# A spectral filter and a low-rank mixer: the low-rank part of u on four row strips of TensorE, two groups at a time

## The chip, the cores and the metric

The kernel runs on one core of a Trainium2 chip. The metric is the device time of one execution in microseconds (us), median of several runs.

## The reference

x is 8 x 3136 x 256 (batch, sequence, channel). A real FFT along the sequence is multiplied by a complex filter and transformed back; then a low-rank mixing over the sequence and an MLP over the channels follow.

```python
X = np.fft.rfft(x, axis=1)
Y = X * (filt_r + 1j * filt_i)[None, :, :]
x = np.fft.irfft(Y, n=x.shape[1], axis=1)
...
xt = x.transpose(0, 2, 1)
h = xt @ U @ V                                  # rank 32
u = x + h.transpose(0, 2, 1)
ch = np.maximum(u @ w_ch1, 0.0) @ w_ch2         # 256 -> 1024 -> 256
return (u + ch).astype(np.float32)
```

## The kernel before

**The transform.** 3136 = 64 x 49. One batch's spectrum goes through four stages: `f1_units` (64-point transform, tile pf, written to DRAM), `load_a` (reads it back in four pieces of eight frequencies, tile a2), `stream` (per step two frequencies: px = transform over 49, products with the filter, pi = transform back, tile esb, to DRAM), and `load_e` (reads back, tile e2). The last 64-point transform is folded into the making of u: e2 is the stationary operand and the constant s2 is streamed. A step of `stream` is one px of two 256-column matmuls, three products on VectorE (`product`: uv, lines 454 and 456), an addition on GpSimd (y), and, two steps later, a pi of two 256-column matmuls with an eviction by ScalarE. Batch 0 goes through a version of its own ahead of everything (`first_f1`, `first_mid`), and the steps of batch 1 use `both_products` (one VectorE operation).

**The low-rank part.** `h1_unit(b)` forms h1 from e2 and the transformed U: 25 matmuls with 32 stationary columns each, on four column strips of TensorE in turn, so that the 128 rows of h1 hold four partial sums of the 32 ranks. `vr` (made once, by `v_units`) holds V four times, one copy per 32 rows. So one matmul over 128 rows with h1 as the stationary operand and vr streamed both adds the partial sums and multiplies by V.

**The mixer.** A batch is cut into groups of four sequence rows of 128 positions, r0 = 0, 4, ..., 20; the 25th half row of two batches makes one odd group after each odd batch. For a group `make_u` builds u, transposed, in two halves of 128 channels (dh): one matmul with h1 and vr, 512 columns, then four with e2 and s2, 128 columns each, all in one bank, evicted to a tile ut. `mm1(gx, t)` forms eighth t of the hidden layer (two 512-column matmuls, relu into h), `mm2(gx, rr)` forms the output of one row (eight matmuls of 256 columns with h as the stationary operand, two of 128 columns that add u), and after every second row VectorE copies it to och, which is written to the output.

**The order of the work** is written out by hand (`manual_schedule`), so each engine works through its instructions in the order of the program. The main loop runs over the groups gx. A group has four steps a; a step has two `mm1` calls (t = 2a, 2a + 1), `run(slot)`, at a = 2 the `make_u` of the next group, the `mm2` call of the group before (rr = a), and `run(slot + 1)`. So a group of four rows has 8 slots, a batch 48. `run` advances what `put` has set for that slot: steps of `stream` (every 1.5 slots for batch 1, 2.87 for batch 2, every 3 for the others: in a batch's own count slots 1, 4, 7, ... 28 and 31, 34, ... 46), pieces of `f1_units` (every 3 slots: 0, 3, ... 18 and 30, ... 45), loads, and `h1_unit` at slot 44. The steps run out in the second half of batch 6; batch 7's groups have none.

**Buffers.** PSUM has eight banks: one "x" (px), one "f" (pi and h1), four "m" (phh of `mm1`, pu of `make_u`, pf), two "o" (po of `mm2`). A bank is given out again when its reader has finished. In SBUF there are four a2, three ut, 18 h, two och. Lines to know: 506 (h1's eviction), 520 to 531 (`u_part`, lines 524 and 529), 544 to 554 (`make_u`), 556 to 568 (`mm1`; VectorE does the relu of t = 4, in the last batch of 1, 4 and 6, ScalarE the others), 570 to 600 (`mm2`), 435 (px), 252 (`v_units`: a 32-row matmul with the constant `sel`, which makes four copies).

The part of the main loop that sets the order:

```python
        for a in range(4):
            if live:
                mm1(gx, 2 * a)
                mm1(gx, 2 * a + 1)
            if full:
                run(slot)
            if a == 2 and gx + 1 < len(groups):
                nxt = groups[gx + 1][0]
                if nxt != groups[gx][0] and nxt % 2:
                    make_odd(nxt - 1)
                make_u(gx + 1)
            mm2(gx - 1, a)
            if full:
                run(slot + 1)
                slot += 2
```

Of the kernel before, what the change touches and what calls it, by code (L numbers as in the profile page):

```python
# [9 lines left out]
F16 = mybir.dt.float16  # L10
# [6 lines left out]
DM = 256  # L17
RANK = 32
ESC = 16.0
NH = 25  # L20
CH = [6, 6, 6, 7]
KG = 8
# [3 lines left out]
def _consts():  # L26
    n, half = SEQ, SEQ // 2
    r = np.arange(NR)
    q = np.arange(NQ)


    w = np.zeros((NQ, NS, 2))
    for s in range(NS):
        w[:, s, 0] = np.cos(2 * np.pi * s * q / NQ)
        w[:, s, 1] = -np.sin(2 * np.pi * s * q / NQ)
    w[:, 0, 1] = (-1.0) ** q
    w = w.reshape(NQ, 64)
    w64 = np.zeros((128, 128))
    w64[:64, :64] = w
    w64[64:, 64:] = w  # L40
    s2 = np.zeros((128, 128))
    s2[:64, :64] = w.T / ESC
    s2[64:, 64:] = w.T / ESC


    t2 = np.zeros((NS, 98, 128))
    g = np.zeros((NS, 128, 98))
    for s in range(NS):
        for j in range(49):
            if j < 25:  # L50
                f = s + 64 * j
                e, sg = np.exp(-2j * np.pi * f * r / n), 1.0
            elif s:
                f = 64 * (j - 24) - s
                e, sg = np.exp(-2j * np.pi * (n - f) * r / n), -1.0
            else:
                f = 32 + 64 * (j - 25)
                e, sg = np.exp(-2j * np.pi * f * r / n), 1.0
            ei = np.conj(e)
            if s:  # L60
                t2[s, :49, j], t2[s, 49:, j] = e.real, -e.imag
                t2[s, :49, 64 + j], t2[s, 49:, 64 + j] = sg * e.imag, sg * e.real
                g[s, j] = np.concatenate([ei.real, ei.imag]) * 2
                g[s, 64 + j] = np.concatenate([-ei.imag, ei.real]) * 2 * sg
            else:
                o = 0 if j < 25 else 49
                t2[s, o:o + 49, j] = e.real
                t2[s, o:o + 49, 64 + j] = e.imag
                g[s, j, o:o + 49] = ei.real * (2 if f else 1)
                g[s, 64 + j, o:o + 49] = -ei.imag * 2  # L70

    t2[0, :, 64] = 0
    t2[0, 49:, 64] = (-1.0) ** r
    g[0, 64] = 0
    g[0, 64, 49:] = (-1.0) ** r
    g *= ESC / n
    gs = np.concatenate([g[:, 64:], g[:, :64]], 1)
    f16 = np.float16
    return (w64.astype(f16), s2.astype(f16), np.eye(128).astype(f16),
            np.tile(np.eye(32), (1, 4)).astype(f16),  # L80
            np.ascontiguousarray(t2.transpose(1, 0, 2).reshape(98, NS * 128)).astype(f16),
            np.ascontiguousarray(np.stack([g, gs], 1).transpose(2, 0, 1, 3)
                                 .reshape(128, NS * 2 * 98)).astype(f16))
# [3 lines left out]
def kernel(  # L87
# [11 lines left out]
    nc = tc.nc  # L99
# [18 lines left out]
    def bank(tag, name):  # L118
        return ps.tile([128, 512], F32, tag=tag, bufs=BUFS[tag], name=name)
# [78 lines left out]
    load_rest()  # L198
    for c in range(2, len(CH)):
        load_x(0, c)  # L200
    sel = cst.tile([32, 128], F16)
    nc.sync.dma_start(sel, sel_d.ap())
    for k, part in enumerate(PARTS):
        if k == 3:
# [43 lines left out]
    def v_units():  # L248

        for r0, n, vp in vps:  # L250
            pv = bank("m", "pv")
            nc.tensor.matmul(pv[:, 0:n], sel[:, :], vp[:, 0:n], start=True, stop=True)
            nc.scalar.copy(vr[:, r0 * 128:r0 * 128 + n], pv[:, 0:n])
            yield

# [61 lines left out]
    def first_a(m):  # L317
        gi, ml = divmod(m, KG // 2)
        if ml == 0:
            st[0].setdefault("a", {})[gi] = sb.tile([98, KG * DM], F16, tag="a2", bufs=4, name="a2")  # L320
        pt = bank("o", "pt")
        for sl in range(2):
            for dh in range(2):
                o = sl * DM + dh * 128
                k = dh * 64 * NR + (2 * m + sl) * 98
                nc.tensor.matmul(pt[0:98, o:o + 128], at[:, k:k + 98], idn[:, :],
                                 start=True, stop=True, skip_group_check=True)
        nc.scalar.copy(st[0]["a"][gi][:, ml * 512:(ml + 1) * 512], pt[0:98, :])  # L328
# [87 lines left out]
        return bass.AP(tensor=t, offset=gi * KG * 2 * RD, ap=[[DM, 98], [2 * RD, KG], [1, DM]])  # L416

    def load_a(b, gi):
        t = sb.tile([98, KG * DM], F16, tag="a2", bufs=4, name="a2")
        nc.sync.dma_start(t.rearrange("p (k d) -> p k d", d=DM), spec(c1[b], gi))  # L420
        st[b].setdefault("a", {})[gi] = t

# [74 lines left out]
    def h1_unit(b):  # L497
        e2 = st[b]["e2"]
        ph = bank("f", "ph")
        for r in range(NH):  # L500
            j = 32 * (r % 4)
            nc.tensor.matmul(ph[j:j + 32, 0:DM], usb[:, r * RANK:(r + 1) * RANK],
                             e2[:, r * DM:(r + 1) * DM], start=(r < 4), stop=(r >= NH - 4),
                             tile_position=(0, j), skip_group_check=True)
        h1 = sb.tile([128, DM], F16, tag="h1", bufs=2, name="h1")
        nc.scalar.mul(h1, ph[:, 0:DM], 1.0 / ESC)  # L506
        st[b]["h1"] = h1
        yield

# [2 lines left out]
    groups = []  # L512
# [4 lines left out]
    uts, hs, pos, ochs = {}, {}, {}, {}  # L517
    odd = {}

    def u_part(b, r0, nr, half, pm, o, dh):  # L520

        e2, h1 = st[b]["e2"], st[b]["h1"]
        k = 64 if half else 128
        nc.tensor.matmul(pm[:, o:o + nr * k], h1[:, dh * 128:(dh + 1) * 128],  # L524
                         vr[:, r0 * 128:r0 * 128 + nr * k], start=True, stop=False,
                         skip_group_check=True)
        for rr in range(nr):
            a = (r0 + rr) * DM + dh * 128
            nc.tensor.matmul(pm[:, o + rr * k:o + (rr + 1) * k], e2[0:k, a:a + 128],  # L529
                             s2[0:k, 0:k], start=False, stop=(rr == nr - 1),  # L530
                             skip_group_check=True)

    def make_odd(b):
        if b % 2 == 0:
            odd[b // 2] = sb.tile([128, 256], F16, tag="odd", bufs=2, name="odd")
        pm = bank("m", "pu")
        for dh in range(2):
            u_part(b, NH - 1, 1, True, pm, dh * 64, dh)
        a = 64 * (b % 2)
        nc.scalar.copy(  # L540
            odd[b // 2].rearrange("p (h q) -> p h q", h=2)[:, :, a:a + 64],
            pm[:, 0:128].rearrange("p (h q) -> p h q", h=2))

    def make_u(gx):
        b, r0, nr = groups[gx]
        if nr == 1:
            make_odd(b)
            uts[gx] = odd[b // 2]
            return
        uts[gx] = sb.tile([128, 1024], F16, tag="ut", bufs=3, name="ut")  # L550
        for dh in range(2):
            pm = bank("m", "pu")
            u_part(b, r0, nr, False, pm, 0, dh)
            nc.scalar.copy(uts[gx][:, dh * 512:(dh + 1) * 512], pm)  # L554

    def mm1(gx, t):
        w = groups[gx][2] * 128
        ut = uts[gx]
        pm = bank("m", "phh")
        for dh in range(2):  # L560
            nc.tensor.matmul(pm[:, 0:w], w1[:, dh * 1024 + t * 128:dh * 1024 + (t + 1) * 128],  # L561
                             ut[:, dh * w:(dh + 1) * w], start=(dh == 0), stop=(dh == 1))
        h = sb.tile([128, 512], F16, tag="h", bufs=18, name="h")
        hs[gx, t] = h
        if t in ((4,) if groups[gx][0] < nb - 1 else (1, 4, 6)):
            nc.vector.tensor_relu(h[:, 0:w], pm[:, 0:w])  # L566
        else:
            nc.scalar.activation(h[:, 0:w], pm[:, 0:w], RELU)  # L568

    def mm2(gx, rr):  # L570
        if gx < 0 or rr >= groups[gx][2]:
            return
        b, r0, nr = groups[gx]
        w = nr * 128
# [29 lines left out]
    def put(slot, gen):  # L604
        sched.setdefault(int(slot + 0.5), []).append(gen)
# [22 lines left out]
    fill = f1_units(1, True)  # L628
    vgen = v_units()
    first_mid(fill)  # L630
    next(h1_unit(0))
    make_u(0)

    steps = [9 + 1.5 * k for k in range(NP)] + [33 + 2.87 * k for k in range(NP)]
# [9 lines left out]
    for b in range(1, nb):  # L644
        for gi in range(NS // KG):
            t = steps[NP * (b - 1) + GP * gi]
            put(t - 9, one(load_a, b, gi))
        put(SB * b - 4, h1_unit(b))
        if b > 1:
            fill = f1_units(b, b == 2)  # L650
            for k in range(NF):
# [4 lines left out]
                if b > 2:  # L656
                    put(steps[NP * (b - 1)] - 68 + 10 * c, one(load_x, b, c))

    for k in range((NH - 1) // 4):
        put(1 + 2 * k, vgen)  # L660

    slot = 0
    for gx in range(len(groups) + 1):
        live = gx < len(groups)
        full = live and groups[gx][2] == 4
        for a in range(4):
            if live:
                mm1(gx, 2 * a)
                mm1(gx, 2 * a + 1)
            if full:  # L670
                run(slot)
            if a == 2 and gx + 1 < len(groups):
                nxt = groups[gx + 1][0]
                if nxt != groups[gx][0] and nxt % 2:
                    make_odd(nxt - 1)
                make_u(gx + 1)
            mm2(gx - 1, a)
            if full:
                run(slot + 1)
                slot += 2  # L680
# [30 lines left out]
```

## Time and profile before

| | |
|---|---|
| median of 3 runs | 557.24 us (557.11 to 557.61) |
| the profiled execution: time, and span from first to last instruction | 560.07 us, 558.3 us |
| TensorE, matmuls (PE) | 529.5 us busy, 4450 matmuls |
| VectorE (DVE) | 366.9 us busy |
| ScalarE (ACT) | 363.1 us busy |
| GpSimd (POOL) | 248.8 us busy |
| mean granted clock of TensorE | 0.988 |

The table is the page's first part. Busy time of PE is the union of its matmuls, which are pipelined: a 512-column matmul lasts 0.379 us (L561) while the next starts earlier. How fast PE works is read from the starts in a timeline, and what it waits for from the pairs of a late start and the end of another engine's operation just before it. In a row of a group the columns are line, engine, operation, output <- inputs, shapes, count, then busy us, mean ns, and the idle time of the engine before it with what ended it.

### The profile page before, as it was taken

What the parts mean: (1) busy time and instruction counts of PE and PEld (TensorE: products, weight loads), DVE (VectorE), ACT (ScalarE), POOL (GpSimd) and SP (SyncE); (2) the same over time, 40 slices, a digit from 0 to 9 for tenths busy, and PEclk for the clock granted to TensorE, in tenths of its full rate; (3) what the DMA queues carried; (4) which work ended last, traced back from release to release, by engine and by line L of the source; (5) the groups of instructions that cost most, each with busy time, mean ns of one, the idle gap of its engine ahead of it and who ended that gap; (6) DMA issues with size and microseconds to landing.
All of it is one profiled execution on the core that took longest, in us unless ns stands there. A gap on an engine that the chain in (4) does not pass through costs nothing.

```text
span 558.3 us, 11590 instructions
## 1 busy us (share of the span) xinstructions
PE 529.5 (95%) x4450; PEld 377.8 (68%) x4450; DVE 366.9 (66%) x531; ACT 363.1 (65%) x731; POOL 248.8 (45%) x357
## 2 busy tenths in 40 slices
PE   4687999999999999999999999999999999999996
PEld 4564467766677767667676766767677767767765
DVE  7875376657777577767777577767777587424342
ACT  3676866767767586767767587677666576654441
POOL 7667440254546455545545465555444334210000
PEclk9969999999999999999999999999999999999998
DMA  8999979769778756786978758786757544541233
GB/s 135 190 188 251 210 160 228 166 155 197 176 184 206 192 135 154 180 201 171 208 177 193 188 138 164 176 208 168 182 150 162 134 116 94 133 90 43 72 77 86
DMA packets 67785, 89.83 MB, mean 161 GB/s; under 512 B 6753, under 2 KB 53378, under 8 KB 66834
## 3 DMA queue, kind: packets, MB, share of 16 engines
q0 software_dynamic: 19152, 50.41, 41.3%
q1 hardware_dynamic: 48498, 38.62, 28.9%
q8 instruction: 35, 0.57, 0.5%
q14 instruction: 20, 0.16, 0.1%
q10 hardware_dynamic: 80, 0.07, 0.0%
HBM read 56.80 MB, written 48.17 MB: 188 GB/s over the span
## 4 chain that ended last, share of the span: by engine, by line
PE 80%; DMA 11%; DVE 4%; ACT 2%; issue 2%; POOL 1%; SPq 0%; ACTq 0%; DVEq 0%; POOLq 0%
PE po L583 29%; PE phh L561 27%; PE pi L471 4%; PE px L435 4%; PE po L587 4%; PE pu L524 4%; PE pu L529 3%; PE pf L401 2%; DMA s<-s2d 2%; DMA xt<-in_x_dram 2%; DMA a<-c 2%; DMA g<-gd 1%; DMA ft<-in_filt_i_dram 1%; DVE uv L456 1%; DVE uv L443 1%
## 5 line engine op out<-in xcount | busy, mean ns | idle before, releaser
L568 ACT ACTIVATE h<-phh 128x512 f16<-128x512 f32 (+1 forms) x350 | 186.2, 575 | 105.4 <-PE phh L561 105.4
L583 PE MATMUL po<-w,h 128*128 128x256 f16 x1568 | 203.2, 273 | 0.0
L561 PE MATMUL phh<-ut,w 128*128 128x512 f16 x768 | 197.5, 379 | 0.3 <-ACT ut L554 0.2
L459 POOL TENSOR_TENSOR y<-uv 128x512 f16<-128x512 f16 x96 | 110.2, 1148 | 150.4 <-DVE uv L456 72.8
L583 PEld LDWEIGHTS <-h 128*128 128x128 f16 x1568 | 150.0, 98 | 35.8
L456 DVE TENSOR_TENSOR uv<-px,ft 64x512 f16<-64x512 f32 x192 | 132.0, 688 | 2.6
L592 DVE COPY och<-po 128x512 f32<-128x512 f32 x96 | 66.4, 692 | 79.7 <-PE po L587 78.2
L561 PEld LDWEIGHTS <-w 128*128 128x128 f16 x832 | 74.4, 97 | 52.7 <-issue 3.1
L454 DVE TENSOR_TENSOR uv<-px,ft 128x512 f16<-128x512 f32 x96 | 66.0, 687 | 55.1 <-PE px L435 53.1
L475 ACT CAST esb<-pi 98x512 f16<-98x512 f32 x112 | 65.7, 587 | 40.0 <-PE pi L471 31.9
L600 POOL DMA_DIRECT2D out_dram<-och x84 | 45.4, 546 | 64.0 <-DVE och L592 64.0
L407 ACT CAST asb<-pf 128x512 f16<-128x512 f32 (+1 forms) x83 | 47.6, 573 | 17.8 <-PE pf L401 17.8
L566 DVE TENSOR_SCALAR h<-phh 128x512 f16<-128x512 f32 (+1 forms) x66 | 42.9, 649 | 20.1 <-PE phh L561 19.6
L554 ACT CAST ut<-pu 128x512 f16<-128x512 f32 x96 | 51.8, 598 | 2.9 <-PE pu L529 2.6
L435 PE MATMUL px<-a,t 98*128 98x256 f16 x256 | 49.9, 277 | 4.1 <-ACT a L328 0.9
L587 PE MATMUL po<-idn,ut 128*128 128x128 f16 x384 | 52.8, 219 | 0.0
L443 DVE TENSOR_TENSOR uv<-px,ft 128x1024 f16<-128x1024 f32 x32 | 38.2, 1219 | 12.7 <-PE px L435 12.4
L529 PEld LDWEIGHTS <-e 128*128 128x128 f16 (+1 forms) x400 | 30.9, 97 | 18.6 <-issue 3.4
L524 PE MATMUL pu<-vr,h 128*128 128x512 f16 (+1 forms) x112 | 39.6, 354 | 1.4 <-ACT h L506 0.5
L529 PE MATMUL pu<-s,e 128*128 128x128 f16 (+1 forms) x400 | 40.3, 218 | 0.5 <-DMA s<-s2d 0.5
L587 PEld LDWEIGHTS <-ut 128*128 128x128 f16 x384 | 37.5, 98 | 4.4
L136 POOL DMA_DIRECT2D xt<-in_x_dram x64 | 34.4, 542 | 8.9 <-DMA xt<-in_x_dram 3.0
(73 smaller groups left out, 364.2 us busy)
## 6 DMA issues: line engine op xcount, KB each, us to landing
out_dram<-och POOLq DMA_DIRECT2D x84, 256.0 KB, 4.2
a<-c SPq DMA_DIRECT2D x28, 392.0 KB
c<-esb SPq DMA_DIRECT2D x28, 392.0 KB
xt<-in_x_dram POOLq DMA_DIRECT2D x56, 192.0 KB, 5.9
c<-asb POOLq DMA_DIRECT2D x42, 192.0 KB, 3.2
e<-c SPq DMA_DIRECT2D x28, 200.0 KB
e<-c SPq DMA_DIRECT2D x28, 192.0 KB
out_dram<-och SPq DMA_DIRECT2D x12, 256.0 KB
```

The source lines that it names most:

```text
L435: nc.tensor.matmul(px[:, sl * DM:(sl + 1) * DM], t2[:, s * 128:(s + 1) * 128], a2[:, (2 * ml + sl) * DM:(2 * ml + sl + 1) * DM], start=Tru ...
L454: nc.vector.tensor_mul(uv[:, 0:512], px[:, :], ft[:, a:a + 512])
L456: nc.vector.tensor_mul(uv[p:p + 64, 512:1024], px[q:q + 64, :], ft[q:q + 64, b:b + 512])
L459: nc.gpsimd.tensor_add(y, uv[:, 0:512], uv[:, 512:1024])
L475: nc.scalar.copy(esb[:, ml * 512:(ml + 1) * 512], pi[0:98, :])
L524: nc.tensor.matmul(pm[:, o:o + nr * k], h1[:, dh * 128:(dh + 1) * 128], vr[:, r0 * 128:r0 * 128 + nr * k], start=True, stop=False, skip_gr ...
L529: nc.tensor.matmul(pm[:, o + rr * k:o + (rr + 1) * k], e2[0:k, a:a + 128], s2[0:k, 0:k], start=False, stop=(rr == nr - 1), skip_group_chec ...
L561: nc.tensor.matmul(pm[:, 0:w], w1[:, dh * 1024 + t * 128:dh * 1024 + (t + 1) * 128], ut[:, dh * w:(dh + 1) * w], start=(dh == 0), stop=(dh ...
L568: nc.scalar.activation(h[:, 0:w], pm[:, 0:w], RELU)
L583: nc.tensor.matmul(po[:, o:o + DM], hs[gx, t][:, rr * 128:(rr + 1) * 128], w2[:, t * DM:(t + 1) * DM], start=(t == 0), stop=False, skip_gr ...
L587: nc.tensor.matmul(po[:, o + dh * 128:o + (dh + 1) * 128], ut[:, dh * w + rr * 128:dh * w + (rr + 1) * 128], idn[:, :], start=False, stop= ...
L592: nc.vector.tensor_copy(och[:, a:(rr + 1) * DM], po[:, 0:(rr + 1) * DM - a])
```

## The change

The four partial sums of h1 are added before the multiplication by V: h1's eviction goes to a tile `part`, and a second piece of `h1_unit`, one slot later, multiplies it by a matrix of 4 x 4 identity blocks (`sel`, now 128 x 128), which leaves the whole h1 in each of the four 32-row strips. With that, a 32-row strip of h1 and of vr is enough for the low-rank part, and `make_u` runs four such matmuls on four row strips of TensorE, into four banks: two halves of two groups. Then the e2 part of the four follows. `make_u` is called once per two groups, ahead of r0 = 0, 8 and 16, at a = 3 and between `mm2`'s calls for rr = 2 and rr = 3; in the group ahead, `mm2` starts at a = 1 instead of a = 0 and does its last two rows at a = 3. One of the four evictions goes to VectorE, and VectorE's relu moves from t = 4 to t = 7 (last batch: 1, 4, 7). There are four ut and three a2 buffers.

```diff
-            np.tile(np.eye(32), (1, 4)).astype(f16),
+            np.tile(np.eye(32), (4, 4)).astype(f16),
...
+        part = sb.tile([128, DM], F16, tag="part", bufs=1, name="part")
+        nc.scalar.mul(part, ph[:, 0:DM], 1.0 / ESC)
+        yield
+
+        ph = bank("f", "ph")
+        nc.tensor.matmul(ph[:, 0:DM], sel[:, :], part[:, :], start=True, stop=True)
         h1 = sb.tile([128, DM], F16, tag="h1", bufs=2, name="h1")
-        nc.scalar.mul(h1, ph[:, 0:DM], 1.0 / ESC)
+        nc.scalar.copy(h1, ph[:, 0:DM])
...
+    def u_rank(b, r0, n, pm, o, dh, j):
+
+        nc.tensor.matmul(pm[:, o:o + n], st[b]["h1"][j:j + 32, dh * 128:(dh + 1) * 128],
+                         vr[j:j + 32, r0 * 128:r0 * 128 + n], start=True, stop=False,
+                         tile_position=(j, 0), skip_group_check=True)
...
     def make_u(gx):
...
+        b = groups[gx][0]
+        pms = [bank("m", "pu") for _ in range(4)]
+        for j in range(4):
+            u_rank(b, groups[gx + j // 2][1], 512, pms[j], 0, j % 2, 32 * j)
+        for j in range(4):
+            g, dh = gx + j // 2, j % 2
+            if dh == 0:
+                uts[g] = sb.tile([128, 1024], F16, tag="ut", bufs=4, name="ut")
+            u_spec(b, groups[g][1], 4, 128, pms[j], 0, dh)
+            (nc.vector.tensor_copy if j == 1 else nc.scalar.copy)(
+                uts[g][:, dh * 512:(dh + 1) * 512], pms[j])
...
-        if t in ((4,) if groups[gx][0] < nb - 1 else (1, 4, 6)):
+        if t in ((7,) if groups[gx][0] < nb - 1 else (1, 4, 7)):
...
-        put(SB * b - 4, h1_unit(b))
+        h1 = h1_unit(b)
+        put(SB * b - 4, h1)
+        put(SB * b - 3, h1)
...
+        nxt = groups[gx + 1] if gx + 1 < len(groups) else None
+        pair = nxt is not None and nxt[2] == 4 and nxt[1] % 8 == 0
         for a in range(4):
...
+            if pair:
+                mm2(gx - 1, a - 1)
+            if a == 2 and nxt is not None and nxt[0] != groups[gx][0] and nxt[0] % 2:
+                make_odd(nxt[0] - 1)
+            if a == 2 and nxt is not None and nxt[2] == 1:
+                make_odd(nxt[0])
+                uts[gx + 1] = odd[nxt[0] // 2]
+            if pair and a == 3:
                 make_u(gx + 1)
-            mm2(gx - 1, a)
+                mm2(gx - 1, a)
+            if not pair:
+                mm2(gx - 1, a)
```

`u_spec` is the e2 part of the former `u_part`, unchanged. In the changed kernel the matmuls of `u_rank` are line 528, those of `u_spec` line 536, the fold is line 510, the evictions to ut line 563.

More of the change, by code (lines that the diff above doesn't have):

```diff
@@ L200 @@
         load_x(0, c)
-    sel = cst.tile([32, 128], F16)
+    sel = cst.tile([128, 128], F16)
     nc.sync.dma_start(sel, sel_d.ap())
@@ L251, in v_units @@
             pv = bank("m", "pv")
-            nc.tensor.matmul(pv[:, 0:n], sel[:, :], vp[:, 0:n], start=True, stop=True)
+            nc.tensor.matmul(pv[:, 0:n], sel[0:32, :], vp[:, 0:n], start=True, stop=True)
             nc.scalar.copy(vr[:, r0 * 128:r0 * 128 + n], pv[:, 0:n])
@@ L319, in first_a @@
         if ml == 0:
-            st[0].setdefault("a", {})[gi] = sb.tile([98, KG * DM], F16, tag="a2", bufs=4, name="a2")
+            st[0].setdefault("a", {})[gi] = sb.tile([98, KG * DM], F16, tag="a2", bufs=3, name="a2")
         pt = bank("o", "pt")
@@ L418, in load_a @@
     def load_a(b, gi):
-        t = sb.tile([98, KG * DM], F16, tag="a2", bufs=4, name="a2")
+        t = sb.tile([98, KG * DM], F16, tag="a2", bufs=3, name="a2")
         nc.sync.dma_start(t.rearrange("p (k d) -> p k d", d=DM), spec(c1[b], gi))
@@ L518, with u_spec @@
     odd = {}
[L520 to L526, printed above, removed]
+    def u_rank(b, r0, n, pm, o, dh, j):
+        nc.tensor.matmul(pm[:, o:o + n], st[b]["h1"][j:j + 32, dh * 128:(dh + 1) * 128],
+                         vr[j:j + 32, r0 * 128:r0 * 128 + n], start=True, stop=False,
+                         tile_position=(j, 0), skip_group_check=True)
+    def u_spec(b, r0, nr, k, pm, o, dh):
         for rr in range(nr):
             a = (r0 + rr) * DM + dh * 128
-            nc.tensor.matmul(pm[:, o + rr * k:o + (rr + 1) * k], e2[0:k, a:a + 128],
+            nc.tensor.matmul(pm[:, o + rr * k:o + (rr + 1) * k], st[b]["e2"][0:k, a:a + 128],
                              s2[0:k, 0:k], start=False, stop=(rr == nr - 1),
@@ L537, in make_odd @@
         for dh in range(2):
-            u_part(b, NH - 1, 1, True, pm, dh * 64, dh)
+            u_rank(b, NH - 1, 64, pm, dh * 64, dh, 0)
+            u_spec(b, NH - 1, 1, 64, pm, dh * 64, dh)
         a = 64 * (b % 2)
@@ L544, in make_u @@
     def make_u(gx):
[L545 to L554, printed above, removed]
+        b = groups[gx][0]
[9 more added lines that the diff above has]
+                uts[g][:, dh * 512:(dh + 1) * 512], pms[j])
     def mm1(gx, t):
@@ L570, in mm2 @@
     def mm2(gx, rr):
-        if gx < 0 or rr >= groups[gx][2]:
+        if gx < 0 or rr < 0 or rr >= groups[gx][2]:
             return
@@ L630 @@
     first_mid(fill)
-    next(h1_unit(0))
+    h1 = h1_unit(0)
+    next(h1)
+    next(vgen)
+    next(h1)
     make_u(0)
@@ L657 @@
                     put(steps[NP * (b - 1)] - 68 + 10 * c, one(load_x, b, c))
-    for k in range((NH - 1) // 4):
+    for k in range((NH - 1) // 4 - 1):
         put(1 + 2 * k, vgen)
@@ L671 @@
                 run(slot)
[L672 to L675, printed above, removed]
+            if pair:
[6 more added lines that the diff above has]
+            if pair and a == 3:
                 make_u(gx + 1)
-            mm2(gx - 1, a)
+                mm2(gx - 1, a)
+            if not pair:
+                mm2(gx - 1, a)
             if full:
```

## The prediction

> **What bounds the kernel now.** I read the page first, for the engines and the clock; the first line is the span, the next gives busy time, the third the granted clock in 40 slices, the last the group of the matmuls that the change rebuilds.
>
> ```profile
> span 558.3 us, 11590 instructions
> ...
> PE 529.5 (95%) x4450; PEld 377.8 (68%) x4450; DVE 366.9 (66%) x531; ACT 363.1 (65%) x731; POOL 248.8 (45%) x357
> ...
> PEclk9969999999999999999999999999999999999998
> ...
> L524 PE MATMUL pu<-vr,h 128*128 128x512 f16 (+1 forms) x112 | 39.6, 354 | 1.4 <-ACT h L506 0.5
> ```
>
> A busy PE need not be a full one, so I read the timeline next, batch 4 at its second `make_u` (start, length, engine, line). Starts give the pace: four L561 matmuls of 512 columns take 331.42 to 332.28, 0.216 us each; eight of 256 and two of 128 columns (one `mm2` call) 333.63 to 334.61, 0.98; px with its pi 0.44. From 60 us on PE runs at this pace nearly everywhere. So each matmul removed is worth its columns, and each new wait of PE costs its length.
>
> ```profile
> 331.42 1.03 PE L561 MATMUL phh<-ut,w 128*128 128x512 f16 x4
> ...
> 332.28 0.38 PE L401 MATMUL pf<-xt,w 128*128 128x512 f16 x1
> ...
> 332.50 0.38 PE L524 MATMUL pu<-vr,h 128*128 128x512 f16 x1
> ...
> 332.54 0.60 ACT L568 ACTIVATE h<-phh 128x512 f16<-128x512 f32 x1 [1.16 <-PE phh L561]
> 332.61 0.69 DVE L592 COPY och<-po 128x512 f32<-128x512 f32 x1
> 332.71 0.39 PE L529 MATMUL pu<-s,e 128*128 128x128 f16 x4
> ...
> 333.19 0.38 PE L524 MATMUL pu<-vr,h 128*128 128x512 f16 x1
> ...
> 333.21 0.68 DVE L566 TENSOR_SCALAR h<-phh 128x512 f16<-128x512 f32 x1
> ```
>
> The second L524 could start at 332.94 and starts at 333.19: its bank is free only when the copy of 332.54 ends. Such a wait of 0.25 stands at nine `make_u` calls between 142 and 395 us. PE's other repeated wait is px. It has one bank ("x"), held until DVE's three products of the step before have ended, as DVE's timeline shows:
>
> ```profile
> 321.77 0.68 DVE L454 TENSOR_TENSOR uv<-px,ft 128x512 f16<-128x512 f32 x1
> 322.46 1.39 DVE L456 TENSOR_TENSOR uv<-px,ft 64x512 f16<-64x512 f32 x2
> 323.88 0.69 DVE L566 TENSOR_SCALAR h<-phh 128x512 f16<-128x512 f32 x1
> ```
>
> These products end at 323.85, and PE's px of 323.91 comes 0.30 late. They take 2.11 us together.
>
> **Rank matmuls.** Removed: 96 matmuls of 0.216, 20.7 us. Added: 24 sets of four row strips. No row strip with a neighbour is in the trace. L252 is a single one (32 rows, 512 columns):
>
> ```profile
> 57.90 1.04 PE L561 MATMUL phh<-ut,w 128*128 128x512 f16 x4
> 58.87 0.39 PE L252 MATMUL pv<-vp,sel 32*128 32x512 f16 x1
> 59.18 1.04 PE L561 MATMUL phh<-ut,w 128*128 128x512 f16 x4
> ```
>
> PE could enter it at 58.77 and enters at 58.87; it leaves at 59.18 instead of 59.09. So going into a strip shape and out of it costs 0.10 each. That strips run together is shown for columns: 25 matmuls of 256 columns (L502) take 308.55 to 309.42, of which 0.10 is the way out; one after the other they would take 25 x 0.109 = 2.73. In fours they start 4 ns apart. I take the same for rows, the nearest row: 0.10 + 0.01 + 0.216 + 0.10 = 0.43, 24 times 10.2 us. Saved: **10.5**. Bounds: free changes of shape would save up to 24 x 0.20 = 4.8 more (3.5 where no wait hides it); strips one after the other take 0.65 more per set, 15.6, of which 5.8 would pass inside waits found below: 9.8 net.
>
> [...]
>
> **Fold.** Eight matmuls of 256 columns: +0.9. ACT's two evictions of 0.38 have a slot each, with an `mm2` of 0.98 between; uncovered they would cost about 0.4 x 8 = 3. At the start the longer chain from h1 to `mm1` puts `mm1` some 0.6 later, but group 1's u is then made as well: 0, bounds -0.6 and +0.6.
>
> **Buffers.** Three a buffers cost nothing: a load is issued 9 slots ahead of its group's first px, and the last px on the buffer that it takes then lies 27 slots ahead of that first px. If not, SP's queue would stand, with the e2 loads behind it. Four ut buffers are what two u at a time need. The odd groups go through the same changes of shape as before: 0.
>
> **The wait that is added.** `make_u` now takes all four "m" banks at once, right behind `mm1`'s t = 7, whose relu is moved to DVE. In the changed program's order the fourth strip waits for that relu in every steady set, and the relu stands behind whatever DVE has. I walk the engines through it with durations of rows above; DVE starts 0.20 (och, 319.36 after 319.16) or 0.27 (product, 335.10 after 334.83) after PE could issue its next matmul, a bank is free 0.06 after its reader ends, DVE's next operation starts 0.60 after an och or relu started.
> Group r0 = 4, time 0 at the px of slot 13, which now follows `mm2`'s second call. PE: px and pi 0.44, t = 6 and 7 0.86, third `mm2` 0.98, change of shape 0.10: the fourth strip could start at 2.38. DVE: och 0.20 to 0.80, products 0.80 to 2.91, relu to 3.60, bank at 3.66. PE waits **1.27**; behind it stand all 16 spectral matmuls, `mm2`'s last call and the next group. Batches 2 to 6 have a stream step there: 6.4.
> Group r0 = 12, px of slot 28 ahead of the second `mm2`: strips at 0.44 + 0.98 + 0.86 + 0.22 (pf) + 0.98 + 0.10 = 3.58; relu after products (0.49 to 2.60) and och (to 3.20) ends at 3.89, bank 3.95: 0.37 four times (batches 1 to 4), 0.58 twice where no pf is left: 2.6.
> Group r0 = 20: relu ahead of the products, no wait. Last batch: no stream, 0.1 twice, 0.2. The other three banks were read by ACT, in time each time: t = 6's relu ends about 1.9 at r0 = 4.
> DVE also takes one ut copy of 0.69 per set from ACT. Its latest is at r0 = 20, behind the products of slot 46: done at 7.74 from the px of slot 43, needed by `mm1` at 7.82. Cost 0; each 0.1 more of delay would cost 0.1 x 6.
>
> **px waits that are added.** Ahead of a `make_u`, `mm2` starts one step later, so the first step has none of its 0.98 between two px. r0 = 12: px of slot 22 to px of slot 25 is 0.44 + 0.98 + 0.86 = 2.28, while DVE does t = 7's relu (0.26 to 0.86) and the products (to 2.97), bank at 3.03: 0.75, six batches, 4.5. r0 = 4: 0.44 + 0.86 + 0.22 + 0.86 = 2.38 against 2.66 to 2.98: 0.28 to 0.60, five batches, 2.2. r0 = 0 of batches 2, 4, 6 loses the `make_u` (0.88) between slots 4 and 7: 1.52 against 2.64, 1.12 where there was 0.31: 2.4. Batch 0, with products of 1.22: about 0.7. In all 9.8. The same walk over the order of before gives the 0.25 at L524 and the 0.30 at px where the trace has them, which is why I trust it.
>
> **Sum.** -10.5 (rank) -2.3 (nine waits of 0.25 go) +0.9 +6.4 +2.6 +0.2 +9.8 = **+7.1**. The profiled execution ran 560.07 with a span of 558.3; I set the sum on its span, 565.4, and so on the median of the runs, 557.24: 564.3, say **564**.
>
> **Rivals.**
> 1. The gain stays: PE's saving arrives whole because DVE, 66% busy, gets to the relu in time. 557.2 - 10.5 - 2.3 + 0.9 = 545. For it: DVE idles between steps, 1.27 before the products of 330.48 and 1.20 before those of 335.10. Against: idle elsewhere does not help an operation that stands behind 2.11 us of products. It decides if the fourth strip's wait is under 0.4 on average. With half of the 19.0 us of waits: 555.
> 2. Row strips do not overlap, since four write all 128 partitions of PSUM: 564.3 + 9.8 = 574. Against: columns do overlap.
> 3. The clock falls. The granted clock was 1.00 from 60 to 553 us with single waits up to 0.84, but 0.50 from 30 to 34 us, where PE was busy 2.35 of 4 us; the r0 = 4 places come near 2.5 of 4. The slow stretch lasted about 10 us, so one costs up to 5: five places, 589. [...]
>
> **How the numbers follow.** Forecast 0.70, own range 560 to 569 (free changes of shape below; waits some tenths longer each above). Whole gain 0.08, half of the waits 0.08, strips in series 0.10, clock 0.04. Range 553 to 575: it leaves out the whole gain and the clock, and the forecast's tails. This kernel's runs tell 0.2% (1.1 us) from no change. Faster 0.08 + 0.06 = 0.14, no change 0.03 (the edges of half the waits and of the forecast), slower 0.83.
>
> **What will show it.** In the timeline after: four strips within about 20 ns where nothing waits (0.43 from the last matmul before to the first L536); at r0 = 4 the fourth strip some 1.3 behind the third, released by DVE's relu; px waits of 0.75 in r0 = 12's first step; granted clock 1.00. The L528 group with no idle before its strips, or px without waits, would make the forecast wrong; strips 0.216 apart would be rival 2.

## The result and the profile after

The changed kernel takes 580.28 us, median of four runs (574.57 to 584.98), against 557.42 for the kernel before beside it. The ratio is 1.036 (95% interval 1.027 to 1.046); it leaves out the run of 584.98, which was a slow one, over 1.5% above the fastest. The prediction had said slower, 564, and no more than 575.

The page of the changed kernel, the lines that answer to those shown of before. The profiled execution ran 578.39 us.

```profile
span 576.6 us, 11645 instructions
...
PE 526.8 (91%) x4458; PEld 369.9 (64%) x4458; DVE 383.6 (67%) x555; ACT 353.4 (61%) x715; POOL 248.8 (43%) x357
...
PEclk9989999999999999989999999999999999989999
```

The span grew by 18.3 us while PE's busy time fell by 2.7, so the loss is waiting. Two digits of the clock that were 9 fell to 8, in slices 18 and 36. What PE waited for (waits of TensorE of the changed kernel: engine, tile, line, what released it, then us in total, times, longest):

```profile
PE px L435 <- DVE uv L456: 8.8, 16, 1.2
PE pu L528 <- DVE h L576: 4.9, 7, 0.9
...
PE ph L502 <- DMA e<-c: 4.5, 4, 1.4
...
PE px L435 <- DMA a<-c: 2.9, 2, 1.6
...
PE ph L502 <- issue: 2.3, 1, 2.3
```

The first two rows are the waits that the prediction walked. The other three are waits for loads, which it priced at nothing. For the last row the view names no releaser, but the trace's semaphore record has the second e2 load landing at 509.20, and the matmul starts at 509.40. The view gives idle time only. For exact lengths I took every start of a matmul against the start before it and the pace of its shape (0.216 us for 512 columns), in both traces, from the first matmul of `mm1` to the last one of the kernel. The differences, us, waits and changes of shape together:

| | predicted | trace |
|---|---|---|
| low-rank part with its waits (-10.5 - 2.3 + 6.4 + 2.6 + 0.2) | -3.6 | -3.3 |
| px waiting for VectorE | +9.8 | +10.4 |
| fold, and a little low-rank work now done ahead of the loop | +0.9 | +0.3 |
| h1's first matmul, waiting for the last e2 load | 0 | +6.9 |
| px waiting for an a load (1.80 and 1.48; before 0.65, at another place, and 0.16) | 0 | +2.6 |
| matmuls at half clock | 0 | about +2.3 |
| start of the loop (55.05 instead of 56.35) | 0 | -1.3 |
| pieces under 0.2 | | about +0.4 |
| sum | +7.1 | +18.3 |

The walked rows came out within 0.6 each. The step that had been walked for r0 = 4 looks like this in batch 4 (timeline of the changed kernel, PE and VectorE: start, length, engine, line):

```profile
340.40 0.68 DVE L454 TENSOR_TENSOR uv<-px,ft 128x512 f16<-128x512 f32 x1
340.90 1.04 PE L593 MATMUL po<-w,h 128*128 128x256 f16 x8
341.10 1.39 DVE L456 TENSOR_TENSOR uv<-px,ft 64x512 f16<-64x512 f32 x2
341.77 0.28 PE L597 MATMUL po<-idn,ut 128*128 128x128 f16 x2
341.98 0.39 PE L528 MATMUL pu<-vr,h 32*128 32x512 f16 x3
342.52 0.69 DVE L576 TENSOR_SCALAR h<-phh 128x512 f16<-128x512 f32 x1
...
343.26 0.37 PE L528 MATMUL pu<-vr,h 32*128 32x512 f16 x1 [0.89 <-DVE h L576]
343.57 1.07 PE L536 MATMUL pu<-s,e 128*128 128x128 f16 x16
```

Three strips start within 0.01 us of each other, all by 341.99. The fourth starts at 343.26, 1.28 late: the relu stands behind three products and ends at 343.21, and the bank is free 0.05 later. 1.27 had been predicted.

Now the part that was not walked: the end of batch 2 in the changed kernel (timeline, the DMA queue of SP and PE; SPq is the issue of a transfer).

```profile
236.05 0.33 SPq L477 DMA_DIRECT2D c<-esb  x1
...
236.49 0.46 SPq L420 DMA_DIRECT2D a<-c  x1
...
241.63 1.66 SPq L427 DMA_DIRECT2D e<-c  x2
...
243.89 0.28 PE L597 MATMUL po<-idn,ut 128*128 128x128 f16 x2
...
245.80 0.38 PE L435 MATMUL px<-a,t 98*128 98x256 f16 x2 [1.63 <-DMA a<-c]
...
248.42 1.65 PE L502 MATMUL ph<-e,usb 128*32 128x256 f16 x25 [1.16 <-DMA e<-c]
250.00 1.59 PE L593 MATMUL po<-w,h 128*128 128x256 f16 x8
```

The spectrum's last piece is written (236.05), read back into e2 (issued 241.63), and used by h1 (248.42). Between write and use lie 12.4 us, and the chain of waits of the changed kernel names them:

```profile
236.05 5.56 DMA c<-esb
242.00 6.28 DMA e<-c
248.42 1.65 PE ph L502 x24
```

The same place before the change (timeline, SP's queue, then PE):

```profile
235.02 0.33 SPq L477 DMA_DIRECT2D c<-esb  x1
235.44 0.47 SPq L420 DMA_DIRECT2D a<-c  x1
240.57 0.78 SPq L427 DMA_DIRECT2D e<-c  x2
```

```profile
236.11 0.38 PE L524 MATMUL pu<-vr,h 128*128 128x512 f16 x1
...
245.25 0.38 PE L435 MATMUL px<-a,t 98*128 98x256 f16 x2
...
246.88 0.92 PE L502 MATMUL ph<-e,usb 128*32 128x256 f16 x25 [0.18 <-DMA e<-c]
```

There it took 11.9 us, and h1 came 0.34 late: the transfers just fitted. This is h1 of batch 3; h1 of batches 2 and 4 to 7 found its e2 landed 0.2 to 1.8 us before. PE's own work between write and h1 was 11.9 - 0.3 = 11.5 us before and 12.4 - 1.3 - 1.8 = 9.3 after. The missing two are a `make_u` with its wait (0.88 + 0.25, at 236.11 above), which is now done with the group ahead, and an `mm2` call of 0.98, which the shifted `mm2` leaves for later. The change took away PE work under which a load had been hidden, and the loads take as long as ever or somewhat longer. Over the seven batches, PE's own work between write and h1 fell by 0.9 to 2.1 us each, while the last e2 load landed 8.1 to 11.7 us after the write's issue before the change and 8.9 to 12.2 after it. And the DMA engines have little room: from the issue of the a load to its px they are busy 0.98 of the time before (235.44 to 245.10) and 0.99 after (236.49 to 245.66).

After two of these waits TensorE ran slower for a while. The stretches of the changed kernel around the longest wait, 2.46 us at 509.40 (columns: stretch and its length, then the busy time of PE, PEld, DVE, ACT and POOL with counts, granted clock, DMA share, GB/s):

```profile
506.00:510.00 4.00, 1.70 (x32) 1.00 (x30) 0.00 (x0) 1.21 (x3) 0.00 (x0) 1.00 0.64 155
510.00:514.00 4.00, 4.00 (x30) 2.25 (x20) 0.69 (x1) 1.02 (x3) 0.00 (x0) 0.57 0.00 0
514.00:518.00 4.00, 4.00 (x44) 3.08 (x43) 1.60 (x3) 2.16 (x4) 0.00 (x0) 1.00 0.00 0
```

PE is full from 510 to 514 but does 30 matmuls at clock 0.57. In the finer record the clock is 0.50 for 3.4 us, from 510.6 to 514.0, and once more from 247.7 to 251.2, where the `mm2` call of 250.00 above takes 1.59 instead of 1.04.

### The profile page after: what moved, and what is told of

It is laid out like the page before. It is cut to its first block, busy times and chain, and to the rows that moved or that the text cites. A ratio compares the mean times of both kernels' runs of the same rounds, so it can differ in the third digit from the quotient of the medians.

```text
span 576.6 us, 11645 instructions
## 1 busy us (share of the span) xinstructions
PE 526.8 (91%) x4458; PEld 369.9 (64%) x4458; DVE 383.6 (67%) x555; ACT 353.4 (61%) x715; POOL 248.8 (43%) x357
## 4 chain that ended last, share of the span: by engine, by line
PE 64%; DMA 15%; DVE 11%; issue 4%; ACT 4%; POOL 1%; SPq 0%; DVEq 0%; ACTq 0%; POOLq 0%
PE po L593 24%; PE phh L571 19%; DVE uv L456 5%; DMA c<-esb 5%; DMA e<-c 4%; PE pu L536 4%; DMA xt<-in_x_dram 4%; PE px L435 3%; PE po L597 3%; PE pi L471 3%; DVE uv L454 3%; PE pf L401 2%; PE pu L528 2%; ACT h L578 2%; PE ph L502 1%
## 5 line engine op out<-in xcount | busy, mean ns | idle before, releaser
L563 ACT CAST ut<-pu 128x512 f16<-128x512 f32 x72 | 37.5, 594 | 39.7 <-PE pu L536 39.7
L435 PEld LDWEIGHTS <-t 98*128 98x128 f16 x256 | 21.4, 99 | 36.8 <-DVE uv L456 18.6
L401 PE MATMUL pf<-xt,w 128*128 128x512 f16 (+1 forms) x91 | 34.1, 376 | 4.0 <-DMA xt<-in_x_dram 2.9
L471 PE MATMUL pi<-y,g 128*98 128x256 f16 x192 | 36.7, 272 | 0.0
```

What stands on the lines that cost most here:

```text
L435: nc.tensor.matmul(px[:, sl * DM:(sl + 1) * DM], t2[:, s * 128:(s + 1) * 128], a2[:, (2 * ml + sl) * DM:(2 * ml + sl + 1) * DM], start=Tru ...
L471: nc.tensor.matmul(pi[0:98, sl * DM:(sl + 1) * DM], g12[:, g:g + 98], y[:, o:o + DM], start=(fi == 0), stop=(fi == nf - 1), skip_group_che ...
```

## The experiments

The theory, stated once the traces had been compared: the extra 11 us beyond the walked waits come from loads whose cover the change shortened. The rivals: the smaller number of a buffers holds the loads back; the strips cost more than their records show; the order of `mm2` and the place of the relu cost more than walked. The runs are in the order in which they were made. Medians are compared with the kernel before beside them, 558.4 to 559.6 us.

**The stream earlier, in the changed kernel.** The steps of batches 2 to 7 come three slots earlier, so every write, read-back and use of a batch has more time before h1 at its old slot.

```diff
-    steps = [9 + 1.5 * k for k in range(NP)] + [33 + 2.87 * k for k in range(NP)]
+    steps = [9 + 1.5 * k for k in range(NP)] + [33 + 2.67 * k for k in range(NP)]
...
-        steps += [SB * (b - 2) + 31 + 3 * k for k in range(NP)]
+        steps += [SB * (b - 2) + 28 + 3 * k for k in range(NP)]
```

> The changed kernel with the stream steps of batches 2 to 7 one step (3 slots) earlier; nothing else. Theory (late loads): the last write of a batch's c2, the load of e2 behind it and h1 follow each other in a fixed time of DMA (5.5 + 6 us in the trace), and the change took about 2.3 us of PE work from between; 3 slots give back about 3.9 us. Then the waits of h1's first matmul on e2 (7.6 us in the changed kernel's trace) fall below 1.5, the two stretches at half clock after 60 us go, and the time falls by 8 to 11 us, to about 570. The waits of the fourth strip (1.28 at r0 = 4) and of px (0.73 at r0 = 12) stay. Rival (the excess over the forecast is PE's new order and its changes of shape): no change, 575 to 585.

Measured: 568.06, ratio 1.015 (1.010 to 1.020), so 12 less than the change (10.2 by the two profiled spans). The waits of TensorE:

```profile
PE px L435 <- DVE uv L456: 9.2, 19, 1.2
...
PE pu L528 <- DVE h L576: 4.7, 6, 0.9
...
PE ph L502 <- DMA e<-c: 2.0, 1, 2.0
```

The walked waits stay. One wait of h1 is left, in batch 1, whose steps were not moved; the a loads and the half clock after 60 us are gone. What is left over before, 8.5 us, is near the 7.1 that the prediction had added.

**Four a buffers.** `bufs=3` of a2 becomes `bufs=4`.

```diff
...
-        t = sb.tile([98, KG * DM], F16, tag="a2", bufs=3, name="a2")
+        t = sb.tile([98, KG * DM], F16, tag="a2", bufs=4, name="a2")
```

> The changed kernel with four a buffers, as before. Theory (late loads): the two waits of px on the a load (1.8 and 1.5 us) come from the shorter way from the load's issue to px, not from the buffers, so they stay, and the time stays within the changed kernel's own spread, 573 to 585. Rival (three buffers hold the load back): both waits go, 3.3 us less, and the load is issued earlier on SP.

Measured: 578.02, 1.034 (1.027 to 1.040), no difference from the change that can be told. px still waits for a loads (1.91 and 0.41, the second shorter than in the change), h1 up to 3.53. The number of buffers is not the cause.

**The relu back at t = 4.**

```diff
-        if t in ((7,) if groups[gx][0] < nb - 1 else (1, 4, 7)):
+        if t in ((4,) if groups[gx][0] < nb - 1 else (1, 4, 6)):
```

> The changed kernel with VectorE's relu at t = 4 again (last batch 1, 4, 6) and t = 7 on ScalarE. Theory: the fourth strip's waits (1.28 five times, 0.37 to 0.58 six times, 0.78 once, about 9.7 us by the starts) go, since t = 4's relu stands ahead of the products; they lie outside the stretch from the last c2 write to h1, so the whole is gained: 8 to 10 us less, about 570. h1's waits stay at 7 to 8 us. Rival (PE would wait for ScalarE's relu of t = 7 instead): 0 to 3 us less.

Measured: 569.90, 1.019 (1.013 to 1.025), some 10 less than the change (8.4 by the spans). The rows of L528 behind VectorE are gone from the waits, but another grew:

```profile
PE px L435 <- DMA a<-c: 8.3, 7, 4.1
```

The longest of these waits, in the timeline of TensorE:

```profile
246.17 0.58 PE L435 MATMUL px<-a,t 98*128 98x256 f16 x2 [4.11 <-DMA a<-c]
```

By the starts it is 4.27, where the changed kernel has 1.80. This is not cover lost: from the issue of that load (234.39 here, 236.49 in the changed kernel) to its px, PE's own work is 7.51 us in both. The load itself was slower, px at 11.8 us after its issue instead of 9.3, with the DMA engines busy all the time (1.00). Why it was slower is not shown. So the strips' waits, 9.7 us by the starts, do belong to the relu, but part of what their removal gave was lost again to loads.

**`mm2` spread otherwise around the pair.** Rows 0 and 1 at a = 0 and 1, rows 2 and 3 on either side of `make_u` at a = 3, so that the first step of the group keeps its `mm2` between two px.

```diff
-            if pair:
+            if pair and a < 2:
-                mm2(gx - 1, a - 1)
+                mm2(gx - 1, a)
...
             if pair and a == 3:
+                mm2(gx - 1, 2)
                 make_u(gx + 1)
-                mm2(gx - 1, a)
+                mm2(gx - 1, 3)
```

> The changed kernel with the mm2 call that is held back ahead of a make_u taken from a = 2 instead of from a = 0: mm2 rows 0 and 1 at a = 0 and 1, rows 2 and 3 around make_u at a = 3. Theory: px of r0 = 12 and r0 = 4 get their mm2 back in between (4.4 and about 1.5 us of waits go), the stretch from the last c2 write to h1 becomes 1 us longer (h1 waits fall by about 1 each, 5 in all, and the a waits by 1 each), the fourth strip's waits change to about 1.04 at r0 = 4 and 0.75 to 0.97 at r0 = 12 (1 us more in all). In all 9 to 13 us less, about 568. Rival (px waits merely move to the next px): 0 to 3 us less.

Measured: 571.30, 1.021 (1.015 to 1.026), 9 less (8.4 by the spans). The px waits of r0 = 12 are gone and the strips wait 1.04 at r0 = 4 and 0.75 to 0.97 at r0 = 12, both as the walk of the order gave. h1 still waits 0.27 to 1.80, and px 0.45 to 1.71 for four a loads.

**The three edits together.** Earlier stream, relu at t = 4, `mm2` spread.

> The changed kernel with all three cures together: stream 3 slots earlier, VectorE's relu at t = 4, mm2 held back at a = 2 instead of a = 0. Theory: what is left of the change is its gain on PE (10.5 and 2.3 us), less the fold (0.9), the px waits of r0 = 0 in even batches (2.4), the smaller px waits and batch 1's wait of h1 (about 2): 7 us below before, 548 to 553. Rival (the transfers between c2 write and h1 are the wall for any faster PE): h1 and px wait for loads again and the time is that of before, 555 to 560.

Measured: 558.36, 0.998 (0.995 to 1.001): no difference from before, and 5 above the upper end of what I expected. The waits that are left are loads again: px on an a load 1.20 (351.62) and 2.04 (368.82), h1 of batch 1 2.3.

**The stream earlier in the kernel before.** The two lines of the first experiment, in the kernel before: is an earlier stream a gain of its own?

> The kernel before with the stream 3 slots earlier. Theory: before's PE has only 0.34 us of such waits outside batch 1, so this is worth nothing there: within 1 us of before, either way. Rival (an earlier stream is a gain by itself, and the 10 us that it gave the changed kernel have nothing to do with the change): several us faster.

Measured: 565.50, 1.009 (1.006 to 1.013). Not the same but slower, which I had not expected. Its longest new waits are of px on a loads, 2.77 at 373.34 and 2.10 at 242.79 by the starts. The second in the timeline, and the clock after it (columns as above):

```profile
242.79 0.38 PE L435 MATMUL px<-a,t 98*128 98x256 f16 x2 [1.94 <-DMA a<-c]
```

```profile
240.00:244.00 4.00, 2.06 (x15) 1.28 (x13) 1.34 (x3) 2.15 (x4) 3.21 (x5) 0.97 0.92 174
244.00:248.00 4.00, 4.00 (x21) 2.33 (x20) 1.35 (x2) 1.68 (x4) 1.15 (x1) 0.61 0.74 203
```

This a load was issued at 231.07 and is used 11.7 us later. Moving the stream moves which load is late; it lets the change's loads land in time, but it is no gain by itself. So the 12 us of the first experiment are not a gain that the kernel before had left lying.

**Whole matmuls in the changed order.** Earlier stream, the order of the change, but the low-rank part by matmuls over 128 rows with vr as before, and no fold.

```diff
...
-        nc.tensor.matmul(pm[:, o:o + n], st[b]["h1"][j:j + 32, dh * 128:(dh + 1) * 128],
-                         vr[j:j + 32, r0 * 128:r0 * 128 + n], start=True, stop=False,
-                         tile_position=(j, 0), skip_group_check=True)
+        nc.tensor.matmul(pm[:, o:o + n], st[b]["h1"][:, dh * 128:(dh + 1) * 128],
+                         vr[:, r0 * 128:r0 * 128 + n], start=True, stop=False,
+                         skip_group_check=True)
```

> The changed order with the stream 3 slots earlier, but with whole 128-row matmuls for the low-rank part and no fold: the strips alone are undone, beside the run 'early' (568.06 us). Theory: a set takes 0.864 instead of 0.424, but where the fourth strip waits for VectorE the first three matmuls pass inside that wait. The 5 sets of r0 = 4 lose nothing (0.1 less, no change of shape), the 6 of r0 = 12 within 0.1 either way, 13 sets lose 0.44: 5.7 - 0.5 + 0.1 - 0.9 (fold) = 4.4 us more than early, about 572.5. Rival (strips are worth the whole 10.5 in any order): 9.6 us more, 577 to 578.

Measured: 570.24, 1.020 (1.015 to 1.024), against 568.06 for the same order with strips, on another chip. The starts of the loop differ between these two profiles (52.8 and 56.1). From the first matmul of `mm1` to the last matmul of the kernel the two differ by 509.6 - 504.7 = 4.9 us. Of this 1.03 is a wait of px for an a load (227.50) that only this run has, and 0.25 a longer wait of h1 in batch 1, so some 3.6 are left for the strips, below the 4.4 expected: the four matmuls run under part of the wait for the fourth bank, so a set without that wait would be worth more.

**Two strips, one group at a time.** The kernel before with the fold and the earlier stream; `make_u` stays where it was and runs its two rank matmuls on two strips.

```diff
...
-        for dh in range(2):
-            pm = bank("m", "pu")
-            u_part(b, r0, nr, False, pm, 0, dh)
+        pms = [bank("m", "pu") for _ in range(2)]
+        for dh in range(2):
+            u_rank(b, r0, 512, pms[dh], 0, dh, 32 * dh)
+        for dh in range(2):
+            u_part(b, r0, nr, False, pms[dh], 0, dh)
...
-        put(SB * b - 4, h1_unit(b))
+        put(SB * b - 5, h1)
+        put(SB * b - 4, h1)
```

> The kernel before in its own order, stream 3 slots earlier, with the fold and with row strips for one group at a time: two strips, two banks. Theory: going into the strip shape and out of it costs 0.10 each, so a set of two takes 0.42 where two whole matmuls took 0.43; 48 of them save 0.6, the fold costs 0.9, h1 is one slot earlier: as before_early, within 1.5 us. Rival (changes of shape are covered by other work): 48 x 0.2 = 9 us less than before_early.

Measured: 575.10, 1.028 (1.024 to 1.032), 10 above the same stream without strips, where I had expected the same. The waits show an error of my placement:

```profile
PE px L435 <- DMA a<-c: 4.0, 2, 2.5
PE ph L502 <- ACT esb L475: 3.4, 5, 0.7
...
PE pu L528 <- ACT h L512: 1.6, 4, 0.5
```

h1 and the fold use the bank that pi uses, and in their new slot h1 stands right behind a pi and waits for its eviction. So the whole time says little. Batch 7 has neither stream nor h1, and there the comparison is clean: 55.12 us with five sets of two strips, 55.05 with whole matmuls. Two strips gain nothing, since the two changes of shape (0.20) eat the one matmul of 0.22 saved.

**More time for the loads alone.** The changed kernel with h1 and the fold a slot later, and the a loads (all but a batch's first) issued 13 slots ahead instead of 9.

```diff
-            put(t - 9, one(load_a, b, gi))
+            put(t - (13 if b > 1 and gi else 9), one(load_a, b, gi))
-        put(SB * b - 4, h1)
-        put(SB * b - 3, h1)
+        put(SB * b - 3, h1)
+        put(SB * b - 2, h1)
```

> The changed kernel with its loads given more time and no stream step moved: h1 and its fold one slot later (slots 45 and 46), the a loads behind the first of batches 2 to 7 issued 13 slots ahead of their px instead of 9. Theory (late loads): h1's waits (0.8 to 2.5, 7.6 in all) lose about 1.2 each and come to about 2, the two a waits (3.3) go, and with the long waits the stretches at half clock after 60 us: 9 to 11 us less than the changed kernel, 568 to 571, as with the earlier stream. The fourth strip's and px's waits on VectorE stay as they were. Rival (the earlier stream helped by where its steps fell among the groups, not by the loads): within 3 us of the changed kernel.

Measured: 573.78, 1.026 (1.020 to 1.031). The waits for a loads fall to one of 0.35 and those of h1 to two, 2.10 and 0.90. Behind the wait of 2.10 the clock fell to 0.50 for 3.4 us once more. And the fold has come behind a pi, and its wait is new:

```profile
PE ph L510 <- ACT esb L475: 3.4, 5, 0.7
...
PE ph L502 <- DMA e<-c: 1.9, 1, 1.9
```

Measured on the starts this is 0.83 to 0.99 five times, 4.3 us, which is about what the result misses of the 568 to 571 expected.

**All four edits, and all but the earlier stream.** The first (`best2` below) has the three edits of before and the loads' one, the second (`best3`) is without the earlier stream.

> The three cures together (stream 3 slots earlier, relu at t = 4, mm2 held back at a = 2) and the loads' cure (h1 one slot later, a loads 13 slots ahead). Theory: best1's remaining waits on loads (a: 1.2 and 2.0, h1 of batch 1: 2.3, and about 1 in batch 1) go; 4 to 6 us below best1, 550 to 555. Rival (the transfers as a whole are the wall): as best1, 557 to 560.

> As best2, with the stream where the change has it (not 3 slots earlier). Theory: gap2 and relu4 leave about 1 us of waits of h1 per batch in the changed stream; the later h1 takes 1.2 of each, the earlier a load the rest: within 2 us of best2. Rival (only the earlier stream frees h1): h1 waits of 1 to 2 us in five batches and slow stretches of the clock, 5 to 9 us above best2.

Measured: 560.38, 1.002 (1.000 to 1.004), and 561.91, 1.003 (1.000 to 1.006). In the first the waits for loads are gone but for 0.65 in batch 1; the fold behind pi takes 0.99 six times in their place. In the second h1 waits 3.05, 1.51, 0.80 and 0.36 besides, and px up to 2.12; but its profiled execution, 566.60, is the longest of its twelve, so these waits are more than a usual run has.

**The same, with h1 later in batch 1 only.** The three edits, the a loads 13 slots ahead, and h1 and the fold one slot later only for batch 1, whose steps are not moved.

```diff
-        put(SB * b - 4, h1)
-        put(SB * b - 3, h1)
+        put(SB * b - (4 if b > 1 else 3), h1)
+        put(SB * b - (3 if b > 1 else 2), h1)
```

> best1 with the a loads 13 slots ahead, and with h1 one slot later for batch 1 alone, so that the fold of the other batches does not come behind a pi in slot 46, where best2 waited 0.99 for the bank of pi. Theory: best1's waits of px on a loads (1.0 and 2.0) go, batch 1's wait of h1 falls from 2.3 to about 0.7 with 0.99 at its fold: 3 to 4 us below best1, 553 to 556, some 0.5% below before. Rival (the runs differ more by the transfers of the first 60 us than by what is left to gain): within 0.3% of before.

Measured: 553.21, median of eight runs (551.58 to 556.72), ratio 0.992 (0.988 to 0.995). This beats both kernels. Its page and the two stretches in which the changed kernel had stood longest (columns as above):

```profile
span 553.0 us, 11651 instructions
...
PEclk9889999999999999999999999999999999999999
```

```profile
240.00:260.00 20.00, 20.00 (x181) 14.18 (x180) 14.26 (x21) 14.71 (x30) 11.20 (x17) 1.00 0.78 192
500.00:520.00 20.00, 20.00 (x163) 13.92 (x162) 9.49 (x14) 8.51 (x15) 1.06 (x2) 1.00 0.24 59
```

PE is full in both and the clock is whole. Some waits for loads are left: 1.05 at h1 of batch 1, 0.81 (224.90) and 1.26 (350.22) at px. Of the span's 5.3 us less than before, 3.1 lie between the first and the last matmul of the loop (493.2 against 496.3) and 2.2 ahead of it. The latter part is not claimed: the loop's start lay anywhere from 52.8 to 57.5 in the profiles of this study.

## Why the prediction was right, and where it failed

**Right: strips, shapes and walked waits.** Four strips start 3 to 4 ns apart; the way into their shape costs 0.10 and out of it 0.10, so a set takes 0.42 where nothing waits (0.43 predicted). Rival 2, strips in series, is out. The fourth strip waits 1.28 (1.27) at r0 = 4, 0.36 and 0.58 (0.37 and 0.58) at r0 = 12; px waits 0.73 (0.75) at r0 = 12 and 1.12 (1.12) at r0 = 0 of batches 2 and 4, 1.34 in batch 6. One wait of the fourth strip, 0.78 in batch 0, was not foreseen. The whole of these rows is +7.1 by the trace and +6.2 by the prediction, so rival 1, the whole gain, is out too: VectorE is 67% busy, and the relu stands behind 2.11 us of products all the same. With the relu at t = 4 the strips' waits go, which shows whose they are.

In the trace the four matmuls of a set take 0.226 us, where four whole ones took 0.864: 3.8x, and 2.0x with the two changes of shape counted (0.42).

**Wrong: the loads were priced at nothing.** The step that failed is the one under "Buffers" and "Fold": it asked whether a buffer is free when a load is issued, and whether h1's evictions have a slot, but not whether a load has landed when its user comes. The prediction had no term for the e2 load ahead of h1, nor for the a load ahead of px. Yet the trace before showed both at the edge: h1 late by 0.34 at 246.88, and px by 0.65 at 137.06 on an a load. (At 119.97 h1 is 0.84 late for another reason: it takes pi's bank, whose eviction ends at 119.92, after e2 has landed at 119.55.) And the prediction named the very work that left: "loses the `make_u` (0.88) between slots 4 and 7" was walked for px, and the same removal of `make_u` and the deferral of an `mm2` call ahead of slot 44 was not. Working: 0.9 to 2.1 us less of PE work per batch under a read-back that had landed between 0.3 us too late and 1.8 us too early. Result: +6.9 at h1, +2.6 at px, 9.5 together. Two runs show the mechanism: more time ahead of h1 takes 10 to 12 us away, and another a buffer takes nothing. The traces show it too: the two a loads that come late, ahead of the px of 245.80 and 379.95, have 7.51 us of PE work between issue and px, where the same two had 9.64 before. The longer wait in the run with the relu moved back is something else: its late load had no less cover, it was slower.

**Wrong in its weight: the clock.** Rival 3 had 0.04 and put the slow stretches at the r0 = 4 places. They did not come there: 1.28 us of waiting, five times, left the clock at 1.00. They came behind the waits for loads, 2.3 us in all, as a consequence of the step that failed.

**The range** ended at 575 since its upper end was made of strips in series, not of late loads. A bound for the loads could have been had from the rows: six uses of e2 after batch 1's, each with up to 2 us of cover lost, 12 us.

**What stays open.** Why the a load in the kernel before with the earlier stream is used only 11.7 us after its issue, and why that of the relu's run takes 11.8, was not taken apart; in both the DMA engines are nearly full (0.93 and 1.00). The 1.3 us at the loop's start is within what that start varies.

## What to carry to other kernels

When a change takes work away from TensorE, or moves it, list the transfers that are in flight meanwhile and the time from issue to use; where the trace shows a wait of some tenths for a load (0.34 and 0.65 us here), the cover is used up, and work removed there can come back as waiting (here 0.9 to 2.1 us less per batch, and 9.5 us more of waiting in all). Removing other waits did not leave the loads' waits as they were (2.9 us at px became 8.3 with the relu moved back), so here such edits only paid together with earlier loads: three of them alone gave nothing against the kernel before, and with the loads' places set right 0.8%. An operation that needs several PSUM banks at once waits for the last of their readers to end (1.28 us for VectorE's relu here): give the last bank to the engine whose queue is shortest at that place.

## What was unexpected of the hardware

In the loop of the changed kernel the clock fell to 0.50 twice, for 3.4 us each (from 247.7 and from 510.6); ahead of the loop of the kernel before it was at 0.50 for 10.2 us (26.3 to 36.6). Such stretches in the loop came with single waits of 2.10 us (the kernel before with the earlier stream, 242.79; mean clock 0.61 from 244 to 248), 2.46 (the changed kernel, 509.40) and 4.27 us (the relu back at t = 4, 246.17; 0.75 and 0.82 from 244 to 248 and on to 252), and with the pair 1.80 and 1.32 (the changed kernel, 245.80 and 248.42). Behind single waits of 2.04 us (the three edits together, 368.82) and 2.64 us (two strips, 251.50) PE kept its pace: the `mm2` call that follows takes 0.99 and 0.98. The changed kernel's five waits of 1.28 left the clock at 1.00. So the length of a wait alone does not decide; what else does is not shown.

A change into the strip shape or out of it cost 0.10 us, for the rows of L528 as for the columns of L502, so both together (0.20) cost nearly as much as one 512-column matmul (0.216). That is why four strips gain (a set takes 0.42 instead of 0.864) and two do not (0.42 instead of 0.43).
